# Gated tiles turned in 32x32 blocks by VectorE and stored with features as rows, in place of TensorE transposes in the last stage

## The chip, the cores and the metric

One core of a Trainium2 chip runs the whole kernel. Its engines work side by side and wait for each other through semaphores: TensorE (PE, with its weight loads PEld), VectorE (DVE), ScalarE (ACT), GpSimd (POOL) and SyncE (SP), which here only issues transfers. The metric is the device time of one launch in microseconds, the median of several runs.

## The reference

Two branches read the same normalised rows and are added to the input.

```python
xn = _layernorm(x)
return x + _A_ref(xn, wqkv, w_phi, wo) + _B_ref(xn, w_in, w_sp, b_sp, w_out)

def _B_ref(x, w_in, w_sp, b_sp, w_out):
    z = _gelu(x @ w_in)                    # 2048 x 1376
    z1 = z[..., :688]
    z2 = _layernorm(z[..., 688:])
    g = w_sp @ z2 + b_sp[:, None]          # 2048 x 2048 times 2048 x 688
    return (z1 * g) @ w_out                # 688 -> 512
```

Branch A is linear attention with 32 heads of 16: keys and queries go through a small matrix and a pair of softmaxes, `num = phi_q (phi_k^T v)` is divided by `den = phi_q sum(phi_k)`, and the result goes through `wo`. The change touches branch B alone: how the gated product `z1 * g`, called u, gets from the place where it is made to the product with `w_out`. There u stands as the operand that must have features on the partitions, so the 688 features of a row tile are needed as rows and its 128 sequence positions as columns.

## The kernel before

The 2048 rows are 16 tiles of 128. Large products are made in fp32r with every operand split into a rounded part h and a remainder l, and three matmuls instead of one (`mm3`, lines 49 to 53): h h, h l, l h. Rounding runs on ScalarE (`round_h`, line 43), the remainder on VectorE (`rest_l`, line 47).

Three stages follow each other. The first projects all tiles, makes the key features and the sums over them, and stores query features (`e_d`) and the raw z1 (`z1_d`) in DRAM. Then z2 is projected and normalised. The second stage, from about 300 to 496 us, is the spatial product `g`, in seven products of half-sized blocks in place of eight (`FORM`, `products`, names P1 to P7). A pair of row tiles i (of 8) is a group of four chunks; each chunk takes two blocks of `w_sp` (`load_a`, two `wf` loads of 256 KB on SP, line 510), makes sums of them and splits all of it into the A operands (`prep_a`: DVE `S` and `A`, ACT `A`), and runs 42 matmuls. The seven sums of a group lie in seven of eight PSUM buffers (`psum("psg", 8)`); `drain` (lines 704 to 717) adds them into a tile `c`, first with an ACT copy of P1 (line 709), then with seven VectorE additions (lines 708 to 713) that free the buffers one after the other. `gate` (line 719) takes z1 through the gelu (ACT, line 722), multiplies by `c` (DVE, line 724), splits the last 48 features into a rounded and a remaining part side by side (lines 727 to 729), and stores the two tiles of the pair, 128 x 736 each, to `u_d` with two GpSimd transfers (line 731). `c` and the z1 tile have one buffer each, so a new drain waits until `c` has been read, and a new load of z1 until the stores have read it.

The last stage runs over pairs of row tiles. `load_u` brings a tile of u back (SP, four buffers, fetched four tiles ahead), `gate_T` turns it with six TensorE transposes into PSUM (`ptu`), from where ACT and DVE split it into `uh` and `ul` (two buffers each) and ACT copies the 96 rest rows to `rt`. `project_u` multiplies these by `w_out` (15 + 2 matmuls into `pout`). In between, attention features are turned (`attend_T`, `ptq`), multiplied by the key sums (`attend`, `po`), split into `oT` and multiplied by `wo` into the same `pout` (`project_o`), which VectorE adds to the input row and SP stores. The query features of later tiles are finished by VectorE meanwhile (`q_fin`: `qtmp`, `et`), and copied to `er` by GpSimd transfers. The gate of the last pair is made inside this stage, after tile pair 8 (`GATE_LAST`), and its drain uses another buffer than `c`.

Each engine works through its own list in order. The lists come from a scheduler that plays the program through when it is built, so the order of the work around the change is its doing, and shifts when an instruction is added. SP's list holds all its loads and stores in one row: an entry that waits holds up those behind it. Two sets of 16 DMA engines' queues are in use beside each other, one for SP's transfers (q1 in the page) and one for GpSimd's (q0); ScalarE's is q10.

Of the kernel before, what the change touches and what calls it, by code (L numbers as in the profile page):

```python
# [10 lines left out]
F32 = mybir.dt.float32  # L11
F32R = mybir.dt.float32r
AF = mybir.ActivationFunctionType
# [5 lines left out]
P = 128  # L19
S, D, H, DH, FH = 2048, 512, 32, 16, 688  # L20
NT = S // P
ND = D // P
FC = FH // 2
NG = 4
NF = 2 * D
KF = FH // P
REM = FH - KF * P
EPS_LN = 1e-5
EPS_DEN = 1e-6
XB = 5  # L30
NP = NT // 2
# [4 lines left out]
def mixer(ctx: ExitStack, tc: tile.TileContext, x, x_t, wv, wqkT, phi_bd, wo, w_in, wst, b_r, w_out, out):  # L36
    nc = tc.nc
    pe, act, dve, pool, sp = nc.tensor, nc.scalar, nc.vector, nc.gpsimd, nc.sync


    def round_h(eng, h, src):
        if eng is act:
            return act.activation(h, src, AF.Copy).ins  # L43
        return eng.tensor_copy(h, src).ins

    def rest_l(l, src, h, eng=None):
        return (eng or dve).tensor_tensor(l, src, h.bitcast(F32), op=ALU.subtract).ins  # L47
# [18 lines left out]
    dram = ctx.enter_context(tc.tile_pool(name="dram", bufs=1, space=DRAM))  # L66
    e_d = dram.tile([NT, P, NF + 2 * H], F32, name="e_d")
    z1_d = dram.tile([NT, P, FH], F32, name="z1_d")
    u_d = dram.tile([NT, P, FH + REM], F32, name="u_d")
    kvT_d = dram.tile([P, D], F32, name="kvT_d")  # L70
    zb_d = dram.tile([P, NF], F32, name="zb_d")

# [91 lines left out]
    with ExitStack() as p0:  # L164
        res = p0.enter_context(left("p0res", 1))
        wk = p0.enter_context(left("p0wk", 2))
        ps = p0.enter_context(psum("p0ps", 4))
# [200 lines left out]
        t = xz.tile([P, 2, FH], F32R, tag="xz", name="xT")  # L368
        xT.append(t)
        x0, pts = xt.pop(0), []  # L370
        for k in range(2):
            pts.append(ps.tile([P, 2, P], F32, tag="mm", name="pt"))
            for c in range(2):
                i = pe.transpose(pts[k][:, c], x0[:, (2 * k + c) * P:(2 * k + c + 1) * P], ident).ins
            keep(pe=i)
        warm_up(2)
        for cs, pt in zip(halves, pts):
            src = pt.rearrange("p a b -> p (a b)")
            i = round_h(act, t[:, 0, cs], src)
# [7 lines left out]
        p = ps.tile([P, D], F32, tag="mm", name="proj")  # L387
        proj(0, wv_h, wv_l, p, (0, 1, 2))
        keep(pe=proj.last)
        pt = turned(1)  # L390
# [4 lines left out]
        p = ps.tile([P, D], F32, tag="mm", name="proj")  # L395
# [18 lines left out]
        p = ps.tile([P, D], F32, tag="mm", name="proj")  # L414
        proj(0, wqk_h[:, 1], wqk_l[:, 1], p, (0, 1))
        keep(pe=proj.last)
        pt = turned(2)
# [227 lines left out]
    for s in range(NT):  # L645
        p = zproj((kv_ps_p, zc, zbp, za)[s % 4], s, w2, (0, 1) if s % 2 == 0 else (1, 0))
        n = s // 2
        if s % 2 == 0:
            z2[n] = zw.tile([P, 4, FC], F32, tag="z2", bufs=2, name="z2")
        z = z2[n][:, 2 * (s % 2):2 * (s % 2) + 2]  # L650
# [32 lines left out]
    gt = mid.enter_context(right("gt", 1))  # L683
    ctx_psg = psum("psg", 8)
    psg = ctx_psg.__enter__()
# [18 lines left out]
    def drain(i, g, cb):  # L704
        g = {k: t[:, :FC] for k, t in g.items()}
        b1, b2 = (bias[:, 2 * i + k:2 * i + k + 1] for k in range(2))
        c11, c12, c21, c22 = (cb[:, k] for k in range(4))
        add = lambda o, p, b, q: dve.scalar_tensor_tensor(o, p, b, q, op0=ALU.add, op1=ALU.add)
        first = act.activation(c12, g["P1"], AF.Copy)
        add(c11, g["P2"], b1, c12)  # L710
        dve.tensor_tensor(c21, g["P6"], c12, op=ALU.add)
        dve.tensor_tensor(c12, g["P5"], c21, op=ALU.add)
        dve.tensor_tensor(c21, g["P7"], c21, op=ALU.add)
        add(c22, g["P5"], b2, c21)
        add(c12, g["P3"], b1, c12)
        drained = add(c21, g["P4"], b2, c21)
        return cb, first.ins, drained.ins

    def gate(i, cb, z):
        cb, first, _ = cb  # L720
        with tc.issue_after(first):
            act.activation(z[:, :, :FH], z[:, :, :FH], AF.Gelu_apprx_tanh)
        zs = z[:, :, :FH].rearrange("p k (j f) -> p k j f", j=2)
        dve.tensor_tensor(zs, zs, cb.rearrange("p (k j) f -> p k j f", k=2), op=ALU.mult)
        rm = slice(KF * P, FH)
        rh = gt.tile([P, 2, REM], F32R, tag="rh", name="rh")
        dve.tensor_copy(rh, z[:, :, rm])
        rest_l(z[:, :, FH:FH + REM], z[:, :, rm], rh)
        dve.tensor_copy(z[:, :, rm], rh.bitcast(F32))
        for k in range(2):  # L730
            pool.dma_start(u_d[2 * i + k], z[:, k])

# [7 lines left out]
            rows += r1 - r0  # L742
        return round_h(act, h, t[:rows]), rest_l(l, t[:rows], h)

    def load_u(i, t):
        sp.dma_start(t.bitcast(F32), u_d[i])
        return t

    def gate_T(ps, tag, z, h, l, rt):
        pt = ps.tile([P, 4, P], F32, tag=tag, name="ptu")  # L750
        for c in range(4):
            pe.transpose(pt[:, c].bitcast(F32R), z[:, c * P:(c + 1) * P], ident_r)
        round_h(act, h[:, :4], pt)
        rest_l(l[:, :4], pt, h[:, :4])
        pt = ps.tile([P, 4, P], F32, tag=tag, name="ptu2")
        pe.transpose(pt[:, 0].bitcast(F32R), z[:, 4 * P:5 * P], ident_r)
        lasts[2] = pe.transpose(pt[:2 * REM, 1].bitcast(F32R), z[:, KF * P:KF * P + 2 * REM], ident_r).ins
        round_h(act, h[:, 4:], pt[:, :1])
        lasts[1] = rest_l(l[:, 4:], pt[:, :1], h[:, 4:])
        lasts[0] = act.activation(rt, pt[:2 * REM, 1], AF.Copy).ins  # L760
        return h, l, rt

    def k_tiles(ap):
        return ap.rearrange("p (k b) -> p k b", b=P)

    def first_gate(i):
        a, b = slot("u_uh", F32R), slot("ul_rt", F32R)
        u = load_u(i, a[:, :FH + REM])
        return gate_T(psg, "g", u, k_tiles(a[:, FH + REM:]), k_tiles(b[:, :KF * P]), b[:2 * REM, KF * P:(KF + 1) * P])

    lasts, wu = [None] * 7, []

# [15 lines left out]
    g, es, ets = {}, {}, {}  # L788
    for n in range(NC):
        i = SEQ[n][0]  # L790
        if n % NQ == 1 and i < NP - 1:
            z = load_z1(i)
        products(n, g)
        if n % NQ == NQ - 1 and i < NP - 1:
            gate(i, drain(i, g, gt.tile([P, 4, FC], F32, tag="c", name="c")), z)
            g = {}
        if n + 3 < NC:
            raw[n + 3] = load_a(n + 3)
        if n + 2 < NC:
            A[n + 2] = prep_a(n + 2, raw.pop(n + 2))  # L800
        if n == NC - 4:
            stage_w()
        if n == NC - 3:
            zs = slot("zb", F32R)
            zb, ident_r = zs[:, :NF].bitcast(F32), zs[:, NF:NF + P]
            round_h(act, ident_r, ident)
            sp.dma_start(zb, zb_d)
            uT = [first_gate(0)]
            ets[2] = load_q(2, slot("et"))
            es[2], last = q_fin(ets.pop(2), slot("qtmp")[:, :NF], zb)  # L810
        if n == NC - 2:
            es[0], es[1] = first_q(0), first_q(1)
            ets[3] = load_q(3, slot("et"))
    cb = drain(NP - 1, g, slot("c").rearrange("p (a b) -> p a b", a=4))
# [4 lines left out]
    gt = p2.enter_context(right("gl", 1))  # L819
    cw = ctx.enter_context(left("cw", 1))  # L820
    wk = ctx.enter_context(left("cwk", 2))
    us, fin = {}, []

    def fetch_u(i):
        return load_u(i, cw.tile([P, FH + REM], F32R, tag="u", bufs=4, name="u"))

    def features(s):
        with tc.issue_after(fin[-1]):
# [5 lines left out]
        es[s] = cw.tile([P, NF], F32R, tag="er", bufs=6, name="er")  # L834
        lasts[6] = pool.dma_start(es[s].bitcast(F32), e).ins

    def gated(z, ps=None):
        return gate_T(*(ps or (pst, "tr")), z, wk.tile([P, KF, P], F32R, tag="uh", name="uh"),
                      wk.tile([P, KF, P], F32R, tag="ul", name="ul"), wk.tile([2 * REM, P], F32R, tag="rt", name="rt"))

    us[1] = fetch_u(1)
    kvT = cw.tile([P, 2 * NG, HP], F32, name="kvT")
    with tc.issue_after(cb[1]), tc.issue_after(cb[2]):
        uT.append(gated(us.pop(1), (psg, "g")))
    ctx_psg.__exit__(None, None, None)
    fin.append(last)
    sp.dma_start(kvT.rearrange("p g t -> p (g t)"), kvT_d)
# [37 lines left out]
    def project_u(i, u):  # L885
        uh, ul, rt = u
        p = pso.tile([P, D], F32, tag="out", bufs=2, name="pout")
        for c in range(KF):
            mm3(p, (uh[:, c], ul[:, c]), wu[c], c == 0, False)
        for k, w in enumerate(wu[KF]):  # L890
            pe.matmul(p, rt, w, start=False, stop=i == NT - 1 and k == 1)
        return p

    def project_o(i, oT, p):
# [41 lines left out]
    for i in range(0, NT, 2):  # L936
        if i:
            p[i] = project_u(i, nxt.pop(i))
            if i + 2 < NT:
                nxt[i + 2] = gated(us.pop(i + 2))  # L940
            with tc.issue_after(lasts[2]):
                oT, _ = attend(fT)
            with tc.issue_after(lasts[3]):
                p[i + 1] = project_u(i + 1, nxt.pop(i + 1))
        else:
            nxt[2] = gated(us.pop(2))
        if i + 3 < NT:
            nxt[i + 3] = gated(us.pop(i + 3))
        for k in range(2):
            project_o(i + k, oT, p.pop(i + k))  # L950
            ahead(i + k)
        if i == 2:
            with tc.issue_after(lasts[6]):
                z = load_z1(NP - 1)
        if i == GATE_LAST:
            with tc.issue_after(lasts[0]), tc.issue_after(lasts[1]):
                gate(NP - 1, cb, z)
            p2.close()
        if i + 2 < NT:
            with tc.issue_after(lasts[4]):  # L960
                fT = attend_T(i + 2)
# [33 lines left out]
```

## Time and profile before

| | |
|---|---|
| runs, median (lowest to highest) | 639.09 us (639.05 to 639.24), 3 runs |
| span of the profiled execution, first to last instruction | 637.5 us |
| granted TensorE clock | 1.000 |
| one group of the spatial product (one gate) | 26.4 us |
| stores of u, issue to landing, median | 4.3 us |
| loads of u, issue to landing, median | 4.4 us |

The page gives no other time for the profiled execution than its span; the runs lie 1.6 us above it. In a row of the timeline stand the start, the length and the engine, then line, operation and tiles (written <- read), the shape on both sides and how many of them follow each other; in brackets the engine's idle time before, and what ended it. Lengths on PE overlap: two matmuls that follow each other are told apart by their starts. In the view of stretches each column is the busy time of an engine with the number of its instructions, then the granted clock, the mean share of the 16 DMA engines, and GB/s. In the DMA view a queue's row has its packets, its megabytes, and the time of its packets as a share of 16 engines over the window.

### The profile page before, as it was taken

To read this page: it belongs to the slowest core of one execution; us is meant where nothing else is said; L and a number is where in the kernel's file an instruction comes from. 1 tells how busy PE (TensorE), PEld (TensorE's weight loads), DVE (VectorE), ACT (ScalarE), POOL (GpSimd) and SP (SyncE) were. 2 spreads that over 40 slices of the span, in tenths; PEclk is the share of its full clock that TensorE was granted. 3 is DMA by queue.
4 is the path that set the end of the run, shared out by engine and by line. 5 is a ranking of instruction groups with operands and counts; after the bars stand their busy time and mean duration, and the time that the engine had idled before them with its cause. 6 is when DMAs were issued, how large, how long until landed. Compare 5 with 4: busy or idle time off the path is not lost.

```text
span 637.5 us, 11610 instructions
## 1 busy us (share of the span) xinstructions
PE 631.8 (99%) x4502; PEld 575.1 (90%) x4502; DVE 510.1 (80%) x924; ACT 278.0 (44%) x463; POOL 95.0 (15%) x184
## 2 busy tenths in 40 slices
PE   8999999999999999999999999999999999999997
PEld 7888888888888999999999999999999777888886
DVE  5999979987978759889977869678696598989522
ACT  5644434443332648886453434434353423323230
POOL 4142222111010024441010010000100001101000
PEclk9999999999999999999999999999999999999999
DMA  8445464354245931002353352533547687794620
GB/s 315 160 100 142 124 174 114 119 139 140 75 116 166 334 119 60 2 1 84 128 191 130 117 184 71 173 130 125 178 150 260 190 312 260 282 305 175 231 67 33
DMA packets 38647, 98.41 MB, mean 154 GB/s; under 512 B 4832, under 2 KB 6112, under 8 KB 38592
## 3 DMA queue, kind: packets, MB, share of 16 engines
q1 hardware_dynamic: 27392, 56.78, 27.1%
q0 software_dynamic: 8896, 35.26, 18.0%
q10 hardware_dynamic: 2304, 5.64, 2.3%
q8 instruction: 35, 0.57, 0.4%
q14 instruction: 20, 0.16, 0.1%
HBM read 56.37 MB, written 26.61 MB: 130 GB/s over the span
## 4 chain that ended last, share of the span: by engine, by line
PE 97%; SPq 1%; DMA 1%; DVE 1%; issue 0%; POOL 0%; POOLq 0%
PE g L53 11%; PE g L52 11%; PE g L51 11%; PE proj L51 7%; PE proj L53 7%; PE proj L52 7%; PE zps L53 6%; PE zps L51 6%; PE zps L52 6%; PE pout L51 5%; PE pout L53 5%; PE pout L52 5%; PE po L877 1%; PE ptq L862 1%; PE kvps L310 1%; PE pt L266 1%
## 5 line engine op out<-in xcount | busy, mean ns | idle before, releaser
L52 PE MATMUL g<-B,A 128*128 128x344 f32 x448 | 143.3, 320 | 0.0
L51 PE MATMUL g<-B,A 128*128 128x344 f32 x448 | 143.1, 319 | 0.0
L53 PE MATMUL g<-B,A 128*128 128x344 f32 x448 | 143.0, 320 | 0.0
L51 PEld LDWEIGHTS g<-B,A 128*128 128x128 f32 x448 | 84.2, 188 | 0.0
L52 PEld LDWEIGHTS g<-B,A 128*128 128x128 f32 x448 | 84.1, 188 | 0.0
L53 PEld LDWEIGHTS g<-B,A 128*128 128x128 f32 x448 | 84.1, 188 | 0.0
L47 DVE TENSOR_TENSOR A<-S,A 128x512 fp32r<-128x512 f32 x64 | 43.9, 688 | 29.8 <-ACT A L43 28.7
L43 ACT ACTIVATE A<-S 128x512 fp32r<-128x512 f32 x64 | 40.1, 630 | 58.4 <-PE g L53 35.1
L111 ACT ACTIVATE e<-e,r_x 128x1024 f32<-128x1024 f32 x28 | 32.2, 1149 | 49.8 <-DVE e L110 49.8
L43 ACT ACTIVATE A<-wf 128x512 fp32r<-128x512 f32 x64 | 33.4, 523 | 41.4 <-PE g L53 37.1
L51 PE MATMUL proj<-wqk_h,xT 128*128 128x512 f32 x128 | 50.9, 398 | 0.0
L53 PE MATMUL proj<-wqk_h,xT 128*128 128x512 f32 x128 | 50.6, 395 | 0.0
L52 PE MATMUL proj<-wqk_l,xT 128*128 128x512 f32 x128 | 50.3, 393 | 0.0
L51 PE MATMUL zps<-w_0h,xT 128*128 128x344 f32 x128 | 41.4, 323 | 0.0
L53 PE MATMUL zps<-w_0h,xT 128*128 128x344 f32 x128 | 41.1, 321 | 0.0
L51 PE MATMUL zps<-w_1h,xT 128*128 128x344 f32 x128 | 41.0, 320 | 0.0
L53 PE MATMUL zps<-w_1h,xT 128*128 128x344 f32 x128 | 40.9, 320 | 0.0
L52 PE MATMUL zps<-w_0l,xT 128*128 128x344 f32 x128 | 40.9, 319 | 0.0
L52 PE MATMUL zps<-w_1l,xT 128*128 128x344 f32 x128 | 40.9, 319 | 0.0
L47 DVE TENSOR_TENSOR A<-wf,A 128x512 fp32r<-128x512 f32 x64 | 35.5, 554 | 5.3 <-ACT A L43 5.0
L114 DVE TENSOR_REDUCE sm<-e 128x64 f32<-128x1024 f32 x28 | 33.9, 1211 | 4.9 <-ACT e L111 4.8
L864 ACT ACTIVATE f<-ptq 128x512 f32<-128x512 f32 x32 | 16.6, 603 | 36.2 <-PE ptq L862 29.1
(215 smaller groups left out, 1436.9 us busy)
## 6 DMA issues: line engine op xcount, KB each, us to landing
wf<-in_wst SPq DMA_DIRECT2D x64, 256.0 KB, 3.3
e_d<-e POOLq DMA_DIRECT2D x16, 544.0 KB, 5.2
et<-e_d SPq DMA_DIRECT2D x16, 544.0 KB, 5.9
zacc<-e POOLq DMA_DIRECT2D x12, 512.0 KB, 4.7
er<-et POOLq DMA_DIRECT2D x12, 512.0 KB, 3.9
u_d<-z1t POOLq DMA_DIRECT2D x16, 368.0 KB, 4.3
u<-u_d SPq DMA_DIRECT2D x15, 368.0 KB, 4.4
z_d<-z1f ACTq DMA_DIRECT2D x16, 344.0 KB, 3.3
```

Source lines behind the costliest of these rows:

```text
L43: return act.activation(h, src, AF.Copy).ins
L47: return (eng or dve).tensor_tensor(l, src, h.bitcast(F32), op=ALU.subtract).ins
L51: pe.matmul(dst, ah, bh, start=start, stop=False)
L52: pe.matmul(dst, ah, bl, start=False, stop=False)
L53: return pe.matmul(dst, al, bh, start=False, stop=stop).ins
L111: act.activation(e, e, AF.Exp, scale=scale)
L114: dve.tensor_reduce(sm, heads(e), axis=AX.X, op=ALU.add)
L266: ins = pe.transpose(pt[:, c], xs[:, c * P:(c + 1) * P], ident).ins
L310: i = pe.matmul(kv_acc[k:k + QP, m // 4], vs[:, m * QP:(m + 1) * QP], e[:, m * HP:(m + 1) * HP], start=first and m < 4 and len(ready) == n ...
L862: pe.transpose(pt[:, a, k].bitcast(F32R), src, ident_r)
L864: lasts[5] = act.activation(f, pt.rearrange("p a k b -> p a (k b)"), AF.Copy).ins
L877: lasts[3] = pe.matmul(po[r][c * QP:(c + 1) * QP, k], kvT[rows, m // 2, cols], fs[m // 4][rows, m // 2 % 2], start=True, stop=True).ins
```

## The change

After the gate VectorE turns the whole pair, 128 x 1472, in blocks of 32 x 32, into the tile `c`, which it has just read. A turned block has features on the partitions and 32 positions along the row. Four SP stores, one for each band of 32 partitions, put the blocks where they belong in `u_d`, which now has features as rows: 736 rows of 128 positions for a tile. Each store moves 32 x 46 pieces of 32 numbers. `load_u` then brings u already turned: five groups of 128 features in one load, pieces of 128 numbers, and the 96 rest rows in a second load straight into `rt`. ScalarE and VectorE split it from SBUF, 640 columns at once, and the TensorE transposes, the PSUM tiles for them and the ACT copy of the rest rows are gone. The last gate has a tile `zt` of its own for the turned pair.

```diff
-    u_d = dram.tile([NT, P, FH + REM], F32, name="u_d")
+    u_d = dram.tile([NT, FU, P], F32, name="u_d")
...
-    def gate(i, cb, z):
+    def gate(i, cb, z, zt):
...
         dve.tensor_copy(z[:, :, rm], rh.bitcast(F32))
-        for k in range(2):
-            pool.dma_start(u_d[2 * i + k], z[:, k])
+        dve.transpose(zt, z.rearrange("p k f -> p (k f)"))
+        dst = u_d[2 * i:2 * i + 2].rearrange("k (j a) t -> a (k j) t", a=BL)
+        for b in range(0, P, BL):
+            sp.dma_start(dst[:, :, b:b + BL], zt[b:b + BL].rearrange("p (m b) -> p m b", b=BL))
...
-    def load_u(i, t):
-        sp.dma_start(t.bitcast(F32), u_d[i])
-        return t
-
-    def gate_T(ps, tag, z, h, l, rt):
-        pt = ps.tile([P, 4, P], F32, tag=tag, name="ptu")
-        for c in range(4):
-            pe.transpose(pt[:, c].bitcast(F32R), z[:, c * P:(c + 1) * P], ident_r)
-        round_h(act, h[:, :4], pt)
-        rest_l(l[:, :4], pt, h[:, :4])
...
-        lasts[0] = act.activation(rt, pt[:2 * REM, 1], AF.Copy).ins
+    def load_u(i, u, rt):
+        sp.dma_start(u, u_d[i, :KF * P].rearrange("(k p) t -> p k t", p=P))
+        sp.dma_start(rt.bitcast(F32), u_d[i, KF * P:])
+        return u, rt
+
+    def split_u(u, rt, h, l):
+        lasts[0] = round_h(act, h, u)
+        lasts[1] = rest_l(l, u, h)
         return h, l, rt
...
-            gate(i, drain(i, g, gt.tile([P, 4, FC], F32, tag="c", name="c")), z)
+            c = gt.tile([P, 2 * FU], F32, tag="c", name="c")
+            gate(i, drain(i, g, c[:, :4 * FC].rearrange("p (a b) -> p a b", a=4)), z, c)
...
-        return load_u(i, cw.tile([P, FH + REM], F32R, tag="u", bufs=4, name="u"))
+        return load_u(i, cw.tile([P, KF, P], F32, tag="u", bufs=4, name="u"),
+                      cw.tile([2 * REM, P], F32R, tag="rt", bufs=6, name="rt"))
...
-                gate(NP - 1, cb, z)
+                gate(NP - 1, cb, z, gt.tile([P, 2 * FU], F32, tag="zt", name="zt"))
```

The lists of the engines move at three places. On SP, in the spatial product, this stood before (`wf` are the blocks of `w_sp`, `wof` and `zb` are loads for the last stage, `u_uh` is the first tile of u, `et` and `eq` are query features):

```order
L510 DMA wf<-in_wst 128x512 x57
L741 DMA wof<-in_w_out 128x512 x2
L510 DMA wf<-in_wst 128x512
L741 DMA wof<-in_w_out 128x512 x3
L741 DMA wof<-in_w_out 48x512 x2
L807 DMA zb<-zb_d 128x1024
L746 DMA u_uh<-u_d 128x736
```

And now, in the same place, from the fifth gate's stores to the end of the stage (ahead of these rows the same pair of rows, four stores and eight `wf`, is repeated gate by gate):

```order
L735 DMA u_d<-c 32x46x32 x4
L512 DMA wf<-in_wst 128x512 x8
L735 DMA u_d<-c 32x46x32 x4
L512 DMA wf<-in_wst 128x512 x5
L745 DMA wof<-in_w_out 128x512 x2
L512 DMA wf<-in_wst 128x512
L745 DMA wof<-in_w_out 128x512 x3
L745 DMA wof<-in_w_out 48x512 x2
L805 DMA zb<-zb_d 128x1024
L735 DMA u_d<-c 32x46x32 x4
L750 DMA u_uh<-u_d 128x5x128
L751 DMA ul_rt<-u_d 96x128
```

The four stores of each gate now stand in SP's list, eight `wf` loads from gate to gate, where they stood in GpSimd's; those of the seventh gate (number 6) stand ahead of the first load of u.

On VectorE, in the spatial product at the end of the second gate (`z1t` is the gated pair, `S` and `A` the operands of a later chunk), the order before was:

```order
L729 COPY z1t<-rh 128x2x48
L47 TENSOR_TENSOR A<-wf,A 128x256
L528 TENSOR_TENSOR S<-wf 128x256
L531 TENSOR_TENSOR S<-wf 128x256
L529 TENSOR_TENSOR S<-S,wf 128x256
```

and is now:

```order
L731 COPY z1t<-rh 128x2x48
L49 TENSOR_TENSOR A<-wf,A 128x256
L530 TENSOR_TENSOR S<-wf 128x256
L533 TENSOR_TENSOR S<-wf 128x256
L732 STREAM_TRANSPOSE c<-z1t 128x1472
L531 TENSOR_TENSOR S<-S,wf 128x256
```

The block transpose stands three instructions behind the gate's last copy, ahead of the rest of the sums for a later chunk.

On PE, in the last stage ahead of the first output product, the order before was:

```order
L891 MATMUL pout<-wu,rt 128x512 x2
L877 MATMUL po<-f,kvT 32x256 x16
L752 MATMUL ptu<-zb,u 128x128 x4
L756 MATMUL ptu_5715<-zb,u 128x128
L757 MATMUL ptu_5715<-zb,u 96x128
L752 MATMUL ptu<-zb,u 128x128 x4
L756 MATMUL ptu_5731<-zb,u 128x128
L757 MATMUL ptu_5731<-zb,u 96x128
L51 MATMUL pout<-woh,oT 128x512
```

and is now:

```order
L55 MATMUL pout<-wu,ul 128x512
L889 MATMUL pout<-wu,rt 128x512 x2
L875 MATMUL po<-f,kvT 32x256 x16
L53 MATMUL pout<-woh,oT 128x512
L54 MATMUL pout<-wol,oT 128x512
```

The transposes of tiles 2 and 3 stood between `po` and the first product with `wo`; now that product follows `po` directly.

More of the change, by code (lines that the diff above doesn't have):

```diff
@@ L27 @@
 REM = FH - KF * P
+FU = FH + REM
+BL = 32
 EPS_LN = 1e-5
@@ L743, in load_w @@
         return round_h(act, h, t[:rows]), rest_l(l, t[:rows], h)
-    def load_u(i, t):
-        sp.dma_start(t.bitcast(F32), u_d[i])
-        return t
-    def gate_T(ps, tag, z, h, l, rt):
-        pt = ps.tile([P, 4, P], F32, tag=tag, name="ptu")
-        for c in range(4):
-            pe.transpose(pt[:, c].bitcast(F32R), z[:, c * P:(c + 1) * P], ident_r)
-        round_h(act, h[:, :4], pt)
-        rest_l(l[:, :4], pt, h[:, :4])
[L755 to L759, printed above, removed]
-        lasts[0] = act.activation(rt, pt[:2 * REM, 1], AF.Copy).ins
+    def load_u(i, u, rt):
[5 more added lines that the diff above has]
+        lasts[1] = rest_l(l, u, h)
         return h, l, rt
@@ L767, in first_gate @@
         a, b = slot("u_uh", F32R), slot("ul_rt", F32R)
-        u = load_u(i, a[:, :FH + REM])
-        return gate_T(psg, "g", u, k_tiles(a[:, FH + REM:]), k_tiles(b[:, :KF * P]), b[:2 * REM, KF * P:(KF + 1) * P])
+        n = KF * P
+        u = load_u(i, k_tiles(a[:, :n]).bitcast(F32), b[:2 * REM, n:n + P])
+        return split_u(*u, k_tiles(a[:, n:2 * n]), k_tiles(b[:, :n]))
     lasts, wu = [None] * 7, []
@@ L835, in features, with gated @@
         lasts[6] = pool.dma_start(es[s].bitcast(F32), e).ins
-    def gated(z, ps=None):
-        return gate_T(*(ps or (pst, "tr")), z, wk.tile([P, KF, P], F32R, tag="uh", name="uh"),
-                      wk.tile([P, KF, P], F32R, tag="ul", name="ul"), wk.tile([2 * REM, P], F32R, tag="rt", name="rt"))
+    def gated(u):
+        return split_u(*u, wk.tile([P, KF, P], F32R, tag="uh", name="uh"), wk.tile([P, KF, P], F32R, tag="ul", name="ul"))
     us[1] = fetch_u(1)
@@ L843, in mixer @@
     with tc.issue_after(cb[1]), tc.issue_after(cb[2]):
-        uT.append(gated(us.pop(1), (psg, "g")))
+        uT.append(gated(us.pop(1)))
     ctx_psg.__exit__(None, None, None)
@@ L890, in project_u @@
         for k, w in enumerate(wu[KF]):
-            pe.matmul(p, rt, w, start=False, stop=i == NT - 1 and k == 1)
+            lasts[2] = pe.matmul(p, rt, w, start=False, stop=i == NT - 1 and k == 1).ins
         return p
```

## The prediction

> **What bounds the kernel now.** I read the page first: the span, the busy time of the engines, and the chain that ended last.
>
> ```profile
> span 637.5 us, 11610 instructions
> PE 631.8 (99%) x4502; PEld 575.1 (90%) x4502; DVE 510.1 (80%) x924; ACT 278.0 (44%) x463; POOL 95.0 (15%) x184
> PE 97%; SPq 1%; DMA 1%; DVE 1%; issue 0%; POOL 0%; POOLq 0%
> ```
>
> TensorE is busy all the time and is the chain. What leaves it shortens the kernel, as long as nothing that feeds it comes later than it does today. So the question is what covers VectorE and the transfers in the two stages concerned: the spatial product (one gate each 26.4 us, 305 to 496 us) and the last stage (496 us on). The view of stretches gives it:
>
> ```profile
> core 0: us, PE busy (x) PEld busy (x) DVE busy (x) ACT busy (x) POOL busy (x), PEclk, DMA share, GB/s
> 332.20:358.60 26.40, 26.40 (x170) 26.40 (x169) 20.38 (x43) 10.82 (x19) 2.16 (x4) 1.00 0.40 135
> 544.00:560.00 16.00, 16.00 (x113) 12.88 (x112) 15.39 (x28) 5.14 (x12) 1.07 (x2) 1.00 0.78 286
> 560.00:576.00 16.00, 16.00 (x116) 12.96 (x115) 13.67 (x23) 5.12 (x12) 1.08 (x3) 1.00 0.89 296
> 576.00:592.00 16.00, 16.00 (x115) 12.96 (x114) 15.83 (x28) 6.30 (x13) 2.67 (x5) 1.00 0.50 185
> ```
>
> In a gate's cycle VectorE has 6.0 us free and the transfers take 0.40 of the DMA engines; in the last stage VectorE has little left and the DMA engines are loaded up to 0.89.
>
> **Removed: the TensorE transposes.** The timeline of PE at the second row tile, start against start:
>
> ```profile
> 495.70 0.32 PE L53 MATMUL g<-B,A 128*128 128x344 f32 x1
> 495.86 0.46 PE L752 MATMUL ptu<-zb,u 128*128 128x128 f32 x4
> 496.15 0.25 PE L756 MATMUL ptu<-zb,u 128*128 128x128 f32 x1
> 496.25 0.23 PE L757 MATMUL ptu<-zb,u 128*96 128x128 f32 x1
> 496.31 0.47 PE L51 MATMUL pout<-wu,u_uh 128*128 128x512 f32 x1
> 496.62 0.40 PE L52 MATMUL pout<-wu,u_uh 128*128 128x512 f32 x1
> 496.85 0.40 PE L53 MATMUL pout<-wu,ul_rt 128*128 128x512 f32 x1
> ```
>
> The six hold PE from 495.86 to 496.31, 0.45 us, and the product behind them takes 0.31 to its follower instead of 0.23: 0.53 us a tile. There are 16 tiles, 8.5 us if each were worth its full price. Two are not:
>
> ```profile
> 505.75 1.09 PE L877 MATMUL po<-f,kvT 64*32 64x256 f32 x32
> 506.87 0.51 PE L752 MATMUL ptu<-zb,u 128*128 128x128 f32 x4
> ...
> 507.94 0.51 PE L752 MATMUL ptu<-zb,u 128*128 128x128 f32 x4 [0.41 <-DMA u<-u_d]
> ...
> 508.44 0.47 PE L51 MATMUL pout<-woh,oT 128*128 128x512 f32 x1
> ...
> 507.57 1.29 DVE L47 TENSOR_TENSOR oT<-po,oT 128x512 fp32r<-128x512 f32 x2 [1.37 <-ACT oT L43]
> ```
>
> Tiles 2 and 3 are turned between `po` and the first output product, while ACT and VectorE still split `oT`: half of it is there at 508.26, and the third product, 0.46 us into the row tile, needs it. Without the turns that product row can start at 507.8, not before: 0.64 us won, the 0.41 us wait for `u` included. In the later pairs the gate's product of the second tile, 17 matmuls at 0.23 = 3.9 us, stands between `po` and the use of `oT`, so nothing is left open there. Sum on PE: tiles 0 and 1, 1.06; tiles 2 and 3, 0.64; the other twelve, 6.4: **8.1 us**. On ACT and VectorE three and two instructions a tile become one each, over 640 columns; today's pairs take 0.77 and 0.88, and I cost the new ones at the same:
>
> ```profile
> 496.36 0.77 ACT L43 ACTIVATE uh<-ptu 128x512 fp32r<-128x512 f32 x2 [3.10 <-PE ptu L752]
> 498.05 0.88 DVE L47 TENSOR_TENSOR ul<-ptu,uh 128x512 fp32r<-128x512 f32 x2
> ```
>
> **Added: one block transpose a gate on VectorE**, 1472 columns. No row has it. Nearest is the gate's own product over 1376 columns:
>
> ```profile
> L724 DVE TENSOR_TENSOR z1t<-z1t,c x8: 1579/1584/1585, 314.6 to 582.8; 128x1376 f32<-128x1376 f32 x8
> 344.62 0.42 DVE L531 TENSOR_TENSOR S<-wf 128x256 f32<-128x256 f32 x1
> 344.95 0.42 DVE L529 TENSOR_TENSOR S<-S,wf 128x256 f32<-128x256 f32 x1
> ```
>
> By it 1.7 us; at half that speed 3.4. Both fit into the 6.0 us free, so it costs PE nothing; with that cover gone it would be 1.7 us a gate. In the new order it stands between those two rows, so it runs from 344.95 to 346.6 in this cycle. The Trainium skill (VectorE: DVE Perf Modes, The three transpose paths) has 311 ns for a 128x128 block of 2-byte data; scaled to 1472 columns that is an estimate of 3.6 us, which is hidden as well.
>
> **Added: the stores.** Two stores of 128 rows become four, from 32 partitions each, of 46 pieces of 128 B: 5888 packets a gate instead of 256, 368 on each of 16 DMA engines. What does a 128 B packet cost? Two windows of the DMA view have little else in them than small packets: the last output halves (1024 B packets), and the load of the bias (64 B) among rows of 2 to 3 KB, with the page's row on queue 10 for the large ones:
>
> ```profile
> DMA packets 81, 0.08 MB, mean 166 GB/s; under 512 B 0, under 2 KB 81, under 8 KB 81
> q1 hardware_dynamic: 81, 0.08, 48.5%
> ...
> DMA packets 311, 0.38 MB, mean 375 GB/s; under 512 B 157, under 2 KB 157, under 8 KB 311
> q1 hardware_dynamic: 311, 0.38, 107.6%
> ...
> q10 hardware_dynamic: 2304, 5.64, 2.3%
> ```
>
> 1024 B stored: 48.5% of 16 engines in 0.5 us, 3.9 us over 81, 48 ns. Queue 10: 2.3% of 16 x 637.5 over 2304, 102 ns for 2.4 KB. In the 1 us window of the bias: 17.2 us, less 154 large ones at 102, leaves 1.5 us for 157 small ones, 10 ns. A straight line between 64 B and 1024 B gives 12.5 ns for 128 B and 28 for 512 B. Bounds: 10 ns, and 48 ns if a store of 128 B is as dear as one of 1 KB. I take 12.5, since only the end of a store differs from the small packets seen: 4.6 us a gate, bounds 3.7 and 17.7.
>
> What waits for them: the transposed tile is `c`, the only buffer, and the next drain begins by writing it; and the weight loads of SP, queued behind the stores, on the same rings.
>
> ```profile
> 346.77 0.33 SPq L510 DMA_DIRECT2D wf<-in_wst  x1
> 357.49 0.42 DVE L528 TENSOR_TENSOR S<-wf 128x256 f32<-128x256 f32 x1
> 357.59 0.46 ACT L709 ACTIVATE c<-g 128x344 f32<-128x344 f32 x1 [0.48 <-PE g L53]
> 362.32 1.06 DVE L708 SCALAR_TENSOR_TENSOR c<-g,bias,c 128x344 f32<-128x344 f32 x2
> L510 SPq DMA_DIRECT2D wf<-in_wst x64: 327/328/1134, 205.0 to 470.9; - x64
> DMA to landing us min/median/max: 2.9/3.3/6.2
> ```
>
> The `wf` issued at 346.77 and its partner are first used at 357.49. A load's shortest landing, 2.9 us, less its 8 packets (0.8) leaves 2.1 us fixed. So with a packet of d ns the stores, issued from 346.6, have landed at 348.7 + 0.368 d = 353.3, 4.3 us before ACT writes `c`; the two loads behind them (8 packets each, 1.4 us together) at 354.7, 2.8 us before their use. Beyond that PE has about 4 us more: a group has eight PSUM buffers for seven products, the fifth product of the next group takes the buffer that the pair at 362.32 frees at 362.9, and PE comes to it at about 367 (the first product of the last chunk ends by 357.5, a chunk is 26.4/4 = 6.6 us, a product a seventh of it). So PE loses nothing up to d = 31 ns, and at 48 ns 10.3 - 4 = 6.3 us in each of six gates. Cost taken: 0.
>
> **Moved: gate 6's stores stand ahead of the first `u` load on SP.**
>
> ```profile
> 480.32 0.34 SPq L807 DMA_DIRECT2D zb<-zb_d  x1
> 480.78 0.35 SPq L746 DMA_DIRECT2D u_uh<-u_d  x1
> ```
>
> They issue at 480.7, so that load lands at 480.7 + 2.1 + 4.6 + 46 x 0.028 = 488.7, is split by 490.3, and PE wants it at 495.3. VectorE goes on with the last drain behind that split, about 1.4 us later than today (it began at 488.22); I take 0.6 us of it as lost. At 48 ns the load lands at 501.8 and PE stands 8 us.
>
> **In the last stage** `u` arrives in 46 packets of 512 B an engine, 1.3 us, where 8 of 2944 B take 0.9: 0.4 us more in each 8 us. `u` is fetched four tiles ahead. The last gate multiplies at 582.8 (its row above); its stores take 4.6 us more on the queue than today's, and the loads of tiles 14 and 15 wait for them, but these are the last two of sixteen rows of some 8 us, not begun before about 619. Cost 0.
>
> Sum: 8.1 - 0.6 = 7.5 us. The span becomes 630.0; the runs stand 1.6 us above the span (639.1 against 637.5), so **631.6 us**.
>
> **Rivals.**
> *Dear packets (slower).* One mechanism: a 128 B store packet takes over 31 ns, so the weight loads and `c` come late and PE runs out of PSUM. At 48 ns: 6 x 6.3 + 8 - 7.5 = +38, 677 us; gain and loss are equal at about 33 ns. For it: nothing under 1 KB is stored to HBM in this trace. Against: the 10 ns of the small loads, and that time falls with size down to 1 KB. The Trainium skill (DMA: Bandwidth & Descriptors, Specifications) speaks for it: below 512 B the DMA engine reads, modifies and writes. Were that a read and a write of 512 B, it would be 2 x 28 = 56 ns by the line above, and about 700 us; no run here shows such a store. 0.15.
> *Dear issue (slower).* SP's 0.33 us for 128 packets may be 2.6 ns a packet: 1472 packets then hold SP 3.8 us, a gate's four stores 15.3. The weight loads issue at 361.9, land 7.7 us late, 3.7 x 6 = 22 lost, 6 more at the first `u`: 659 us; it decides from some 2.1 ns a packet. Against it: stores and loads of 32 rows take no less.
>
> ```profile
> L741 SPq DMA_DIRECT2D wof<-in_wo x16: 366/419/431, 495.9 to 502.9; - x16
> ```
>
> 0.09, and 0.03 for other losses.
> *Half the gain.* In the last stage VectorE, 15.4 to 15.8 of 16 us busy in two of the stretches, or the transfers at 0.89 become the bound as PE runs 7% faster there; then of the 6.4 us some 3 to 4 go, and 635 to 636 remains. Against it: VectorE has 2.3 us left in the stretch between. 0.17.
>
> **How the numbers follow.** Forecast 0.50 plus an odd 0.01 for more than that; with half the gain 0.68 is faster by more than 0.2% (1.3 us, about what a measurement of this kernel tells from no change); 0.05 within it; slower 0.15 + 0.09 + 0.03 = 0.27. The range begins at the sum with nothing lost on the way, 639.1 - 8.1 and 2.0 more for splits cheaper than today's pairs and for waits that go with them, 629, and goes into the slower cases until 2 in 10 is left out: 648. The forecast's own range is 629 to 634.
>
> **What would show it.** Right: no `ptu` on PE, its busy time down by 8 us, no idle time before `g` and none at 495 us; four store instructions on SP of under 0.5 us each; the stores landing within 7 us; VectorE's transpose at 1.6 to 1.8 us. Wrong: ACT `c<-g` or VectorE `S<-wf` waiting for a DMA, PE idle at the start of each group, SP instructions of microseconds, or PE idle before `pout` in the last stage behind VectorE's `oT` or `ul`.

## The result and the profile after

| | before | the change |
|---|---|---|
| runs, median (lowest to highest) | 639.08 us (639.05 to 639.24), 4 runs | 642.51 us (642.13 to 643.36), 4 runs |
| span of the profiled execution | 637.5 us | 641.6 us |
| granted TensorE clock, mean | 1.000 | 0.995 |

The change is slower by 0.5%, clear of the noise: ratio 1.0054, 95% interval 1.0040 to 1.0068. The forecast was 631.6 us. From the page of the changed kernel, the busy time and the chain that ended last:

```profile
span 641.6 us, 11420 instructions
PE 626.9 (98%) x4406; PEld 567.6 (88%) x4406; DVE 517.2 (81%) x916; ACT 269.8 (42%) x431; POOL 86.0 (13%) x168
PE 94%; DMA 2%; DVE 2%; issue 1%; SPq 0%; ACT 0%; POOL 0%; DVEq 0%; ACTq 0%; POOLq 0%
```

PE has 96 instructions fewer, 6 for each of 16 tiles, but is busy for only 4.9 us less, and the chain has passed from PE to DMA and VectorE for some 4%. Where, the view of stretches shows (a group of the spatial product, the change of stage in two parts, four pairs of the last stage):

```profile
core 0: us, PE busy (x) PEld busy (x) DVE busy (x) ACT busy (x) POOL busy (x), PEclk, DMA share, GB/s
385.00:411.40 26.40, 25.78 (x164) 25.49 (x163) 21.18 (x44) 10.31 (x18) 1.06 (x2) 1.00 0.53 129
498.60:504.80 6.20, 0.36 (x4) 0.10 (x2) 4.75 (x9) 0.00 (x0) 0.00 (x0) 0.89 1.01 355
504.80:511.30 6.50, 6.50 (x17) 5.10 (x18) 3.52 (x7) 0.74 (x1) 0.00 (x0) 0.58 0.51 139
528.00:592.00 64.00, 64.00 (x425) 50.07 (x425) 59.81 (x97) 21.27 (x37) 5.86 (x11) 1.00 0.78 263
```

The last stage is full, as before. A group of the spatial product has 0.6 us of holes, the change of stage stands for 6 us, and then TensorE runs for 6.5 us at a granted clock of 0.58. The timeline of PE there, and the view of waits:

```profile
498.62 0.32 PE L55 MATMUL g<-B,A 128*128 128x344 f32 x1
504.78 0.77 PE L53 MATMUL pout<-wu,u_uh 128*128 128x512 f32 x1 [5.84 <-DVE c L715]
505.34 0.63 PE L54 MATMUL pout<-wu,u_uh 128*128 128x512 f32 x1
505.77 0.63 PE L55 MATMUL pout<-wu,ul_rt 128*128 128x512 f32 x1
```

```profile
DVE S L530 <- DMA wf<-in_wst: 29.6, 6, 5.9
ACT c L711 <- DMA u_d<-c: 12.0, 4, 3.8
PE pout L53 <- DVE c L715: 5.8, 1, 5.8
PE g L53 <- DVE c L715: 2.3, 4, 0.7
```

**The bill.** The last g product starts at 498.62 (495.70 before), the first output product 6.16 us later (0.61 before), `po` of the first pair 11.96 us after that (9.44), and from there to the last PE instruction it is 121.16 us (127.98). So the last stage won 6.8 us from `po` on. With tiles 0 and 1, whose turns stood ahead of `po`, the gain is 7.9 us (the 1.1 us of these two read from the last run below, which has no loss there). Against it stand 3.5 us lost in the spatial product, 6.0 in the gap, and 2.6 by the clock (11.96 less the 9.36 of that last run): 12.1 - 7.9 = 4.2 us, the difference of the spans.

**How the first loss arises.** SP, GpSimd and VectorE at the second gate in the timeline of the change, then GpSimd in that of before:

```profile
346.25 0.33 SPq L512 DMA_DIRECT2D wf<-in_wst  x1
348.55 6.76 SPq L735 DMA_DIRECT2D u_d<-c  x4
355.41 13.35 SPq L512 DMA_DIRECT2D wf<-in_wst  x6
349.05 1.07 POOL L692 DMA_DIRECT2D z1t<-z_d  x2 [26.97 <-DMA wf<-in_wst]
361.63 0.43 DVE L530 TENSOR_TENSOR S<-wf 128x256 f32<-128x256 f32 x1 [4.21 <-DMA wf<-in_wst]
```

```profile
344.56 1.08 POOL L731 DMA_DIRECT2D u_d<-z1t  x2 [18.40 <-DVE A L47]
351.23 1.08 POOL L690 DMA_DIRECT2D z1t<-z_d  x2 [5.59 <-issue]
```

Before, the load of the next z1 waited until the stores had read their tile, 5.6 us behind them. Now the transposition frees the z1 tile, and the load, two transfers of 344 KB, starts 0.5 us after the first store. SP needs 6.76 us to issue the four stores, and `wf`, wanted at 357.4, is there at 361.6. The DMA view, 1 us of the stores alone (349 to 350), 1 us of both (351 to 352) and the 3.7 us in which z1 passes (350.95 to 354.65) (packets, MB, share of 16 engines; q1 is SP's queue, q0 GpSimd's):

```profile
q1 hardware_dynamic: 631, 0.08, 53.2%
...
DMA packets 57, 0.09 MB, mean 88 GB/s; under 512 B 42, under 2 KB 42, under 8 KB 57
q0 software_dynamic: 15, 0.08, 85.2%
q1 hardware_dynamic: 42, 0.01, 6.1%
...
q0 software_dynamic: 158, 0.70, 72.2%
q1 hardware_dynamic: 1024, 0.13, 23.2%
```

Alone, 631 packets take 53.2% of 16 us, 13.5 ns each: the price of the forecast. Beside z1's packets of 5504 B only 42 pass in the 1 us from 351, and 1024 in the whole 3.7 us. z1's own take 13.6 / 15 = 0.9 us each in that 1 us, but 42.7 / 128 = 0.33 us over the whole load (30 of the 158 are of 4 B); before, where nothing under 2 KB was stored beside them, it was 22.3 / 104 = 0.21 us (2 us of the same view, before):

```profile
q0 software_dynamic: 104, 0.50, 69.7%
```

The Trainium skill (DMA: Bandwidth & Descriptors, Queues, rings and completion order) says that an engine takes turns between its queues by whole packets; by that a queue of 128 B packets gets few bytes beside one of 5.5 KB. The trace agrees that the small ones get few bytes, 0.13 MB against 0.70 in the 3.7 us. It does not show turns one by one (1024 small packets to 128 large ones), and the rule does not explain why the first large ones take four times as long.

### The profile page after: what moved, and what is told of

The parts are those of the page before. It is cut to its first block, busy times and chain, and to the rows that moved or that the text cites. A ratio compares the mean times of both kernels' runs of the same rounds, so it can differ in the third digit from the quotient of the medians.

```text
span 641.6 us, 11420 instructions
## 1 busy us (share of the span) xinstructions
PE 626.9 (98%) x4406; PEld 567.6 (88%) x4406; DVE 517.2 (81%) x916; ACT 269.8 (42%) x431; POOL 86.0 (13%) x168
## 4 chain that ended last, share of the span: by engine, by line
PE 94%; DMA 2%; DVE 2%; issue 1%; SPq 0%; ACT 0%; POOL 0%; DVEq 0%; ACTq 0%; POOLq 0%
PE g L53 10%; PE g L54 10%; PE g L55 10%; PE proj L55 7%; PE proj L53 7%; PE proj L54 7%; PE zps L55 6%; PE zps L53 6%; PE zps L54 6%; PE pout L53 6%; PE pout L54 5%; PE pout L55 5%; PE po L875 2%; DMA wf<-in_wst 1%; PE ptq L860 1%; PE kvps L312 1%
## 5 line engine op out<-in xcount | busy, mean ns | idle before, releaser
L45 ACT ACTIVATE A<-wf 128x512 fp32r<-128x512 f32 x64 | 31.7, 515 | 20.1 <-PE g L55 10.0
L530 DVE TENSOR_TENSOR S<-wf 128x256 f32<-128x256 f32 x32 | 13.4, 420 | 29.6 <-DMA wf<-in_wst 29.6
```

The costliest lines, as they stand in the source:

```text
L530: dve.tensor_tensor(sums[:, 0], b[:, 0], b[:, 1], op=ALU.add)
```

## The experiments

All but the first compute what the change computes. Ratios are to the kernel before. "Gap" runs from the start of the last g product to that of the first `pout`; "wo" from the start of the last product of `po` to that of the first with `wo` (1.12 in the change, where PE waits 0.74 us for ScalarE's `oT`); "half" counts the products some 0.43 us apart in place of 0.23. The last four columns are of the profiled execution.

| run | edit to the change | median us | ratio (95%) | last g | gap | wo | half |
|---|---|---|---|---|---|---|---|
| the change | | 642.51 | 1.0054 (1.0040 to 1.0068) | 498.62 | 6.16 | 1.12 | 11 |
| e1 | large pieces | 635.31 | 0.9934 (0.9917 to 0.9950) | 497.21 | 2.21 | 1.12 | 7 |
| e2 | z1 behind the stores | 636.73 | 0.9967 (0.9954 to 0.9980) | 495.38 | 2.40 | 1.21 | 7 |
| e3 | z1 behind two wf | 637.72 | 0.9979 (0.9970 to 0.9987) | 495.12 | 3.65 | 1.59 | 7 |
| e4 | 7th gate's stores later | 640.23 | 1.0010 (0.9996 to 1.0024) | 496.14 | 1.34 | 3.11 | 0 |
| e5 | all stores by GpSimd | 639.52 | 1.0010 (0.9996 to 1.0024) | 501.02 | 1.38 | 1.12 | 0 |
| e6 | e2 and e4 | 636.97 | 0.9963 (0.9951 to 0.9975) | 495.21 | 0.16 | 4.39 | 12 |
| e7 | e3 and e4 | 637.42 | 0.9972 (0.9962 to 0.9982) | 495.62 | 0.16 | 4.18 | 10 |
| e8 | 7th gate's by GpSimd | 636.10 | 0.9957 (0.9940 to 0.9974) | 497.43 | 1.23 | 1.49 | 0 |
| e9 | e2 and e8 | 634.55 | 0.9923 (0.9910 to 0.9936) | 495.37 | 0.16 | 2.50 | 7 |
| e10 | e9, oT first | 632.74 | 0.9901 (0.9886 to 0.9916) | 495.13 | 0.15 | 1.12 | 0 |

Where transfers are late, single executions of one kernel differ by up to 5 us (e4: 636.48 to 641.91; its profile, and so its row's last four columns, is of the fastest), those of the kernel before by 1 us (one, of 923 us, left out). So differences of 1 us between medians are read with care.

**e1: large pieces.**

```diff
-            sp.dma_start(dst[:, :, b:b + BL], zt[b:b + BL].rearrange("p (m b) -> p m b", b=BL))
+            sp.dma_start(dst[b:b + BL], zt[b:b + BL])
```

> The same four stores a gate on SyncE, in the same place and of the same bytes, but each partition's row goes out as one piece of 5888 B instead of 46 pieces of 128 B (so u's pieces stand in the wrong places in DRAM, and the last stage multiplies scrambled values). Theory A (number of small pieces): the loss comes from the 1472 pieces of a store, which hold the queue about 8 us a gate beside the load of z1. Without them the stores land within 5 us, no row of VectorE S waits over 1 us for wf, the last g product stands at 495.5 to 496.5 us, the gap before the first pout is under 2 us and the time is 630 to 633 us. Theory B (the transposition of 1.7 us on VectorE, or the stores' place on SyncE ahead of wf, is what is late): the last g product stays at 498 us or later, the gap at 4 us or more, and the time at 638 to 643 us.

In this profile the first g product already starts at 285.81 (283.57 in the change), 2.2 us late for a reason outside the edit (TensorE waits in the first 12 us and gets a stretch at half clock: granted 0.91 over the first 20 us, 1.00 in the change); less that, the last g stands at 495.0, and no `S` waits for `wf`. So the number of pieces makes the loss of the spatial product, not the transposition or the place on SP: theory A there (beside the load of z1, as e2 and e3 show next). The gap, 2.21, and the time, 635.3, missed the expectation: a third of the gap stays, and the first u and et are still behind stores. The clock has its part in the time: the two of six executions at a granted clock of 1.0 took 633.1 and 633.3 us.

**e2 and e3: the load of z1 in SP's list, right behind the stores, or two wf later.**

```diff
-        if n % NQ == 1 and i < NP - 1:
+        if n == 1:
             z = load_z1(i)
...
+        if n % NQ == NQ - 1 and i + 1 < NP - 1:
+            with tc.issue_after(load_a.last):
+                z = load_z1(i + 1, sp)
```

In e3 the condition is `n % NQ == 2 and 0 < i < NP - 1`, and the tile loaded that of group i.

> The loads of z1 of groups 1 to 6 are issued by SyncE directly behind the gate's four stores, on the same queue, instead of by GpSimd beside them. Theory A1 (the stores share the 16 DMA engines with the z1 load, which the transposition releases at the same moment): the stores now land in 4.6 to 6 us instead of 8, but z1 (some 3.7 us of queue) stands between them and wf, so wf lands as late as before; the last g product stays within 1 us of 498.6, and the time within 3 us of 642.5. Theory A2 (the stores are slow by themselves, 21 to 24 ns a packet whatever runs beside them): the stores still take 7.5 us or more, wf comes 3 to 4 us later still, and with six gates the last g product moves to 505 us or later, the time to 650 us or more.

> As the run with z1 behind the stores, but the first two loads of wf stand ahead of z1 in SyncE's list: stores, wf x2, z1 x2, wf x6. Theory A1 (collision with z1): the stores land in 4.6 to 6 us with nothing beside them, the two wf right behind; no VectorE S waits over 1.5 us for wf at the start of a group, the last g product stands at 495.5 to 496.5 us, VectorE is 3 to 6 us earlier at the seventh gate and the gap before the first pout falls from 5.6 us to 0.5 to 3 us: 631 to 636 us. Theory A2 (the stores are slow by themselves): stores 7.5 us or more, S waits for wf as before, 640 us or more.

A2 falls: the stores take 5.5 to 6.5 us from first to last packet in both (7.7 to 8.8 in the change, the first six gates each). In e2, 1 us in which they run alone at their full rate:

```profile
q1 hardware_dynamic: 1139, 0.14, 96.7%
```

Both lose nothing in the spatial product, with `wf` waits of 7.7 us in six gates (e2) and 1.0 us (e3) instead of 29.6. For e2 that was not expected: `wf` should have landed as late as in the change, since z1 had only moved from beside the stores to behind them. But it landed 2.3 us earlier, 1.0 of it because this gate itself is earlier, SP issuing stores and z1 in 6.5 us:

```profile
347.59 3.78 SPq L735 DMA_DIRECT2D u_d<-c  x4
351.42 2.54 SPq L692 DMA_DIRECT2D z1t<-z_d  x2
354.07 17.90 SPq L512 DMA_DIRECT2D wf<-in_wst  x8
359.35 0.43 DVE L530 TENSOR_TENSOR S<-wf 128x256 f32<-128x256 f32 x1 [1.52 <-DMA wf<-in_wst]
```

The account that fits these rows is VectorE's free time. It had 6.0 us a cycle, the transposition takes 1.7, 4.3 are left. Waits of 1.3 us fit into that, and the transposition comes every 26.4 us. Waits of 4.9 (29.6 over six) don't, and in the change it ends at 348.5, 376.2 and 404.0, every 27.7 us: VectorE falls back by over 1 us a gate, and PE behind it by 3.5 us over the stage. What stayed high in both runs is the gap; e3 missed its expectation by it (3.65 us where at most 3 was expected, 637.72 us where at most 636 was).

**e4 to e7: the seventh gate's stores behind the first loads of the last stage, and all stores by GpSimd.**

```diff
+            store = gate(i, drain(i, g, c[:, :4 * FC].rearrange("p (a b) -> p a b", a=4)), z, c)
+            if i < NP - 2:
+                store()
...
             ets[3] = load_q(3, slot("et"))
+            with tc.issue_after(load_q.last):
+                store()
```

And for e5 alone, which has none of these lines:

```diff
-            sp.dma_start(dst[:, :, b:b + BL],
+            pool.dma_start(dst[:, :, b:b + BL],
```

> Only the four stores of the seventh gate are moved on SyncE, behind the loads of the first u tile, its rest rows, two et and two eq; everything else as in the change. Theory L (the 5.6 us gap and the half clock after it come from these stores, behind which the first u, et and eq wait): those loads issue at about 482 to 484 us, the gap falls under 2 us, the granted clock stays at 1.0 in 496 to 512 us, and the loss of 2.9 us in the spatial product stays: 633.5 to 636.5 us. Theory M (VectorE's own lateness, 5 us by then, makes the gap): the gap stays at 4 us or more and the time at 639 us or more.

> The change with all 32 stores of the turned tiles issued by GpSimd instead of SyncE (the engine that stored them before), nothing else. Theory P (the place on SyncE's queue is what hurts: wf, the first u and et stand behind 5888 small packets): no VectorE S waits over 1.5 us for wf, the first u loads issue at 480 to 483 us, the gap before the first pout is under 1.5 us, the granted clock stays at 1.0 and the time is 629 to 633 us, even if a gate's stores take 10 us beside wf. Theory D (the small pieces are dear wherever they are issued; GpSimd writes its own descriptors): a gate's stores take over 11 us, ScalarE's c waits for them, z1 behind them comes late, and the time is 640 us or more.

> z1 behind the stores on SyncE, and the seventh gate's stores behind the first loads of the last stage: both edits together. If the two losses are separate (stores beside z1 in the spatial product; the seventh gate's stores ahead of the first u, et and eq), they add up: last g product at 495 to 496 us, gap under 1.2 us, granted clock 1.0, the first product with wo 2 to 3 us late as in the run with the late stores alone: 629.5 to 632.5 us. If VectorE's work, not the loads, makes the gap, it stays at 2 us or more and the time at 634 us or more.

> As the run before, but with z1 behind the first two wf loads. By the runs with one edit each: spatial product as there (last g at 495 to 496 us), gap under 1.2 us, 630 to 634 us; z1 right behind the stores was the better place by 1 us, and that should show again.

The profiled execution of e4 bears theory L out (gap 1.34, clock 1.0, 636.48 us), but it is the fastest of twelve: ten have a granted clock of 0.994 to 0.997, and the median misses the time by 3.7 us. What the profile shows late (3.11 at `wo`) is that the stores now stand ahead of the sixteen `wof` loads, and the first product with `wo` waits; that the slower executions lose by the same wait is not shown. e6 shows the wait pure: gap 0.16, but then

```profile
504.95 0.63 ACT L45 ACTIVATE woh<-wof 128x512 fp32r<-128x512 f32 x1 [1.54 <-DMA wof<-in_wo]
506.69 0.63 ACT L45 ACTIVATE woh<-wof 128x512 fp32r<-128x512 f32 x1 [1.11 <-DMA wof<-in_wo]
508.56 0.74 ACT L45 ACTIVATE uh<-u 128x640 fp32r<-128x640 f32 x1 [1.24 <-DMA u<-u_d]
509.20 1.07 ACT L45 ACTIVATE oT<-po 128x512 fp32r<-128x512 f32 x2
```

4.39 us at `wo` and 12 products at half clock behind it. So e6 and e7 met their expected gap and missed their times; moving the stores moved the wait. That e2's place for z1 is 1 us better than e3's did not show again (636.97 and 637.42, intervals overlap). e5 fits neither theory wholly. GpSimd isn't held long by 1472 pieces (0.9 us a store), and its queue packs them into packets of 3584 and 4096 B. But a gate's stores then take 7.6 to 8.9 us from first to last packet, no less than in the change, and 10.4 to 12.1 from first issue to last landing in the spatial product; ScalarE's `c` waits 15.8 us for them in four gates (12.0 in the change), and the last g comes at 501.0. The gap was cured as theory P said, the spatial product was not.

**e8 to e10: only the seventh gate's stores by GpSimd; with e2; and oT split ahead of the later u.**

```diff
+            (pool if i == NP - 2 else sp).dma_start(dst[:, :, b:b + BL],
...
+            with tc.issue_after(attend.act), tc.issue_after(ins):
+                nxt[2], nxt[3] = gated(us.pop(2)), gated(us.pop(3))
```

> The change, with the seventh gate's four stores alone issued by GpSimd instead of SyncE, so that neither the first u, et and eq nor the sixteen wof loads behind them stand behind 5888 small packets. Theory L (the seventh gate's place on SyncE makes the gap, and, when it is moved behind the first loads, the wof loads late): the spatial product keeps its loss (last g at 498 to 499 us), u loads issue behind VectorE's sums within 1 us of zb, the gap before the first pout is 0.3 to 2 us and the wait before the first product with wo about 1.1 us as in the change: 633 to 636.5 us. Theory M (VectorE is late itself by 5 us): the gap stays at 3 us or more: 638 us or more.

> Both cures together: z1 behind the stores on SyncE, and the seventh gate's stores on GpSimd. If the two places on SyncE's queue are the whole loss, nothing is left of it: last g at 495 to 496 us, gap under 1 us, granted clock 1.0 behind it, wait before the first product with wo 1.1 us, and the forecast's sum comes out: 629.5 to 632 us. If something else of the change costs time, it stays above 633 us.

> Both cures, and ScalarE and VectorE split oT of the first pair before they split the u of tiles 2 and 3 (in the change those splits stand ahead of oT in both lists, and wait for u, which SyncE issues behind the sixteen wof loads). Theory W (what is left above the forecast is this wait, 2.5 us before the second product with wo, and the lower clock that follows it): the wait falls under 1.3 us, the granted clock stays at 1.0, and the time is 629.5 to 632 us. Theory X (the sum of the forecast was too high by itself): the wait falls or not, and the time stays within 1 us of 634.5.

e8: the seventh gate's place is worth 6.4 us by the medians, and theory L holds (the last g, 497.43, and "wo", 1.49, lie a little off what was expected). VectorE's lateness alone is 1.1 us of the gap (1.23 against 0.16 in e9). e9: the two cures add up, last g and gap as expected, but 634.55, 2.5 us over: ScalarE's list has the split of tile 2's u ahead of `oT`, and that u, issued behind the `wof` loads, lands late, and a stretch at half clock follows (7 products; the one execution of five at a granted clock of 0.999 took 632.65 us). e10 turns the two round. Waits of PE on the two, e9 and then e10:

```profile
PE pout L53 <- ACT oT L45: 2.1, 1, 2.1
```

```profile
PE ptq L863 <- DMA er<-et: 1.2, 1, 1.2
PE pout L53 <- ACT oT L45: 0.7, 1, 0.7
```

The clock stays at 1.0 and the time falls to 632.74, theory W by its signs, 0.7 us over its range (five executions each, 632.65 to 635.12 and 631.61 to 634.04). In its profile a single wait of 1.2 us for `er`, at 546 us, is left; without it the span of 631.0 would be the forecast's 630.0 within 0.2 us. e10 beats both kernels: 0.9901 of before, interval 0.9886 to 0.9916.

## Why the prediction was wrong

- **8.1 us leave PE: right.** 7.9 were measured, 0.57 and 0.46 for tiles 0 and 1. "In the last stage ... Cost 0" held too: from the fourth pair on a pair takes 15.9 us instead of 16.9 (`po` to `po`), and PE waits for nothing between 528 and 592. With that *half the gain* fell.
- **The transposition at 1.7 us, hidden: right in size.**

```profile
L732 DVE STREAM_TRANSPOSE c<-z1t 128x1472 f32<-128x1472 f32 x7 | 11.9, 1705 | 0.0
```

  But it took 1.7 of VectorE's 6.0 us, and the forecast went on as if the waits for `wf` had all of it and the PSUM buffers' 4 us besides.
- **12.5 ns a packet: right, 13.5.** So *dear packets* fell as a price, neither 48 nor 56 ns came, although its signs are what came: `c` and `S` waiting for DMA.
- **"The stores, issued from 346.6, have landed at 348.7 + 0.368 d = 353.3 ... Cost taken: 0": this step failed.** It took a queue's time as packets by price, on idle DMA engines, and that much comes out where it is so: in e2 the stores of the first six gates have landed 6.8 to 8.0 us after the first issue, 6.7 forecast. But the transposition frees the z1 tile earlier too, and so sets two transfers of 344 KB beside the stores; they took 8 us from first to last packet and 9.4 to 10.4 from issue to landing, their issue held SP for 6.8 us, and `wf` came 4.2 us late in place of 2.8 early. The term put at 0 cost 3.5 us on PE. e2 and e3 remove that collision and the loss with it.
- ***Dear issue*: wrong as a mechanism, near in effect.** A store's issue costs 0.32 us at its shortest, 1472 pieces or not. The last of a gate's four takes up to 4.4 us, and in e2, where the stores are through sooner, no store of the seven gates takes over 2.7; so it seems to be held while those before it drain, which was not tried apart:

```profile
L735 SPq DMA_DIRECT2D u_d<-c x28: 322/1004/4421, 320.5 to 489.7; - x28
```

- **"I take 0.6 us of it as lost": this term was mis-sized, 6.0.** SP, then VectorE, at the end of the spatial product:

```profile
487.47 4.57 SPq L735 DMA_DIRECT2D u_d<-c  x4
492.13 0.65 SPq L750 DMA_DIRECT2D u_uh<-u_d  x1
...
493.89 0.37 SPq L480 DMA_DIRECT2D et<-e_d  x1
...
497.15 0.83 DVE L49 TENSOR_TENSOR ul_rt<-u_uh 128x640 fp32r<-128x640 f32 x1 [4.61 <-ACT u_uh L45]
500.01 1.23 DVE L487 TENSOR_TENSOR qtmp<-et,zb 128x1024 f32<-128x1024 f32 x1 [2.03 <-DMA eq<-e_d]
501.27 1.22 DVE L488 TENSOR_REDUCE et<-qtmp 128x64 f32<-128x1024 f32 x1
502.40 0.57 DVE L710 SCALAR_TENSOR_TENSOR c<-g,bias,c 128x344 f32<-128x344 f32 x1
...
504.12 0.52 DVE L715 TENSOR_TENSOR c<-g,c 128x344 f32<-128x344 f32 x1
```

  The forecast followed u alone. But the features' loads stand behind it on the same queue, and their product and sum, 2.4 us, stand on VectorE ahead of the drain that frees PSUM for `pout`. In e2, where VectorE is not late, u is there at 490.4 (488.7 forecast), the features at 493.0, and the drain starts at 495.4 instead of 491.2; the gap is 2.40 us there. So the place on the queue is worth some 2.3 us by itself, and the rest of the 6.0 is lateness from the term before: the change has these times 6 to 7 us later than e2, its last g only 3.2.
- **Not in the forecast: the clock.** It stood at 0.50 from 503.46 to 510.28 in the change, and the gap made 2.6 us more by that.

## What to carry to other kernels

Price a new transfer together with what the same edit releases: a tile that comes free earlier starts its next load earlier, and the two meet on the same engines. In an in-order queue follow everything that stands behind the long entry, not the next user alone, up to the instruction on which the bottleneck engine waits; here moving the stores cured one wait and made the next, until they left that queue. Count what an engine has free once: time given to a new instruction is no longer there to cover waits.

## What was not expected of the hardware

- Small and large packets on two queues of the same engines slow each other: 42 of 128 B and 15 of 5504 B in 1 us, 1024 and 128 in the 3.7 us of the large ones, against some 1100 of the small in 1 us alone. Why the first large ones take 0.9 us is open; it was not tried apart.
- SP's queue moved each piece of 128 B as a packet of its own (47104 in the trace for 32 stores), GpSimd's packed the same pieces into up to 4096 B, and was still not faster beside other loads.
- The granted clock falls in stretches of one length. Within the work every stretch at 0.50 lasts 3.41 us (e1, e2, e3, e9) or twice that (the change, e6, e7), and it does not begin with the gap: in e2 PE is back at 497.78 and the clock falls at 499.25. Cut each of the twelve profiles into steps of 3.41 us on whose borders the clock's changes lie. Of the steps at full clock, all eight with 1.52 us of PE idle or more were followed by one at 0.50, and none of the 2175 with 1.41 us or less was. In e4 a wait of 2.74 us fell on two steps, 1.41 and 1.33 us of it, and cost no clock. Two steps of e2, then two of e4 (the clock of the step after them is 1.00 too), in the columns of the stretches above: PE's busy time comes first, the clock third from the end:

```profile
495.84:499.25 3.41, 1.47 (x6) 1.24 (x7) 3.40 (x11) 0.13 (x1) 0.00 (x0) 1.00 0.83 249
499.25:502.66 3.41, 3.41 (x10) 2.63 (x9) 2.07 (x3) 0.60 (x1) 0.00 (x0) 0.50 0.48 136
...
506.04:509.45 3.41, 2.00 (x37) 0.95 (x35) 1.39 (x2) 1.19 (x2) 0.00 (x0) 1.00 0.68 197
509.45:512.86 3.41, 2.08 (x9) 1.61 (x10) 2.59 (x4) 2.45 (x4) 0.00 (x0) 1.00 0.99 286
```

  The Trainium skill (TensorE: Matmul & The Clock Gate, What's actually happening) gives an idle window of about 3.4 us that runs free of the program. The trace agrees with the length and with its running free; that 1.52 us of idle time in 3.41 suffice differs from a window that is idle throughout.
